# Two kv products one slot later, and a split of a small load, in a linear-attention and MLP kernel

## The chip, the cores and the metric

One core of a Trainium2 chip. The time is device microseconds (us) of one launch; each kernel was launched three times or more, and medians are quoted. Ratios are computed as the mean time of one kernel's runs over the mean time of the other's runs of the same rounds, so they are not quite the ratio of the medians quoted beside them; the bracket is a 95% interval. The experiments ran in three jobs on three chips, so times are compared within a job; traces are compared by times counted from a common event.

A trace is one execution. Times read from a trace count from its first instruction.

## The reference

Eight batches of 576 tokens with eight heads of 64. Per batch and head `kv = k^T v` (64x64), then `out = q kv`, a root-mean-square norm per head times `g_norm`, then a layer norm times `g_ln`, an MLP 512 -> 2048 -> 512 with a ReLU, and a residual:

```python
kv  = einsum('bhsd,bhse->bhde', k, v)
out = einsum('bhsd,bhde->bhse', q, kv)
x   = out / sqrt(mean(out*out, -1) + 1e-6) * g_norm          # then heads side by side: 512 columns
xn  = (x - mean(x)) / sqrt(var(x) + 1e-6) * g_ln
y   = x + relu(xn @ w_ch1) @ w_ch2
```

## The kernel before

TensorE works almost without a pause through the MLPs, `mm1` (into 2048) and `mm2` (back to 512), batch after batch. The attention of later batches is woven in between. The weaving is by hand: an agenda maps slots to pieces of work, and `tick()`, called once per group of MLP matmuls, emits what stands at the current slot. In `mm2` a slot is four 128x512 matmuls. The order so written is the order of the instructions on each engine.

```python
def load_batch(b, *after):                 # GpSimd: the loads of a batch, behind small copies ("gates")
    for element in after:
        nc.gpsimd.tensor_copy(gate, element)
    load(k_in[b % NB], k, b)
    load(v_in[b % NB], v, b)
    load(q_in[b % NB], q, b)

def turn_q_dma(b):                         # transposed q of a batch
    q_p = kv_in.tile(...)
    nc.vector.tensor_copy(q_p..., q_in[b % NB])                        # VectorE, L203
    q_t = qt_pool.tile([128, JJ, HP, 128], bf16, tag="qt", name="qt")
    nc.sync.dma_start_transpose(q_t..., q_p...)                        # SyncE, L205
    qts[b] = q_t

def kv_of(b):                              # 40 small matmuls, L246, then two copies on ScalarE
    ...

class Tile:                                # 128 tokens of one batch
    def o(self): ...                       # TensorE, L271: q (transposed) times kv
    def sq(self): ...                      # ScalarE
    def red(self): ...                     # VectorE; root (rms): ScalarE; y, x, xc: VectorE, xc reads g_ln_sb
    def turn(self, on_pe): ...             # xT: the DMA transpose that mm1 reads, SyncE, L352

# ... cut: the plan of batches 0 to 2 ...
for b in range(3, B):
    s = 32 * b
    at(47 if b == 3 else s - 60,
       lambda b=b: load_batch(b, qts[b - 1][:1, J, HP - 1, 127:],
                              *([blks[2][2][:1, nK - 1, 511:]] if b == 4 else [])))
    d = -41 if b == 3 else -45
    at(s + d, lambda b=b: kv_of(b))
    at(s + d + 1.7, lambda b=b: turn_q_dma(b))
    for j in range(J):
        o = s + d + (11 if b == 3 else 13) + 5 * j
        plan_tile(o, lambda b=b, j=j: main_tile(b, j), o + 6, False)
    if b % 2:
        plan_tile(s - 14, lambda b=b: rem_tile(b), s - 8, False)
    at(s + 14, lambda b=b: rstd_of(b))
```

`plan_tile(s, ...)` puts o, sq and red at slot s, y, x and xc two slots later. "kv 3" below is `kv_of(3)`, "qT 4" the transposed q of batch 4, "the q copy" the VectorE copy ahead of it.

The other place is the load of `g_ln` (512 floats) to four partitions, from which a shuffle spreads it to all:

```python
nc.vector.memset(gl_row, 0.0)
nc.sync.dma_start(
    gl_row[0:128:32, :],
    bass.AP(tensor=moe_g_ln.tensor, offset=moe_g_ln.offset,
            ap=[[0, 4], list(moe_g_ln.ap[0])]))
# ... cut ...
nc.vector.stream_shuffle(g_ln_sb, gl_row, [0] * 32)
```

Of the kernel before, what the change touches and what calls it, by code (L numbers as in the profile page):

```python
# [14 lines left out]
def kernel(  # L15
# [19 lines left out]
    Dm = H * D  # L35
# [48 lines left out]
    gl_row = work.tile([128, Dm], f32, tag="sq", name="gl_row")  # L84
# [11 lines left out]
    def load_batch(b, *after):  # L96
# [5 lines that stand above are left out]
# [15 lines left out]
    def pairs(t, hp0, hp1):  # L117
# [21 lines left out]
    nc.vector.memset(gl_row, 0.0)  # L139
    nc.vector.memset(gn_row, 0.0)  # L140
    nc.sync.dma_start(
        gl_row[0:128:32, :],
        bass.AP(tensor=moe_g_ln.tensor, offset=moe_g_ln.offset,
                ap=[[0, 4], list(moe_g_ln.ap[0])]))
    nc.sync.dma_start(
        gn_row[0:128:32, :],
        bass.AP(tensor=g_norm.tensor, offset=g_norm.offset,
                ap=[[0, 4], list(g_norm.ap[0])]))
# [52 lines left out]
    def turn_q_dma(b):  # L201
        q_p = kv_in.tile([128, JJ, H, D], bf16, tag="qp", bufs=2)
        nc.vector.tensor_copy(q_p.rearrange("p j h d -> p h j d"), q_in[b % NB])  # L203
        q_t = qt_pool.tile([128, JJ, HP, 128], bf16, tag="qt", name="qt")
        nc.sync.dma_start_transpose(  # L205
            q_t.rearrange("p j hp t -> p (j hp) t"), q_p.rearrange("p j h d -> p (j h d)"))
        qts[b] = q_t
# [31 lines left out]
    def kv_of(b):  # L239
        kv_ps = ps_m.tile([128, HP, D], f32, tag="misc", name="kv_ps")  # L240
        kvp = held[b] = kv_pack[b % 4]
        for hp in range(HP):
            for j in range(JJ):
                for hh in range(2):
                    h = 2 * hp + hh
                    nc.tensor.matmul(kv_ps[hh * D:hh * D + D, hp, :],  # L246
                                     lhsT=k_in[b % NB][:, h, j, :], rhs=v_in[b % NB][:, h, j, :],
                                     start=(j == 0), stop=(j == JJ - 1))
        nc.scalar.copy(kvp[:D, :, :D], kv_ps[:D])  # L249
        nc.scalar.copy(kvp[D:, :, D:], kv_ps[D:])  # L250
# [104 lines left out]
    def main_tile(b, j, pool=None, tag="ops"):  # L355
        q_t, kvp = qts[b], held[b]
        if b not in blks:
            blks[b] = new_block("main", 3)
        return Tile([(slice(0, 128), lambda hp: q_t[:, j, hp, :], kvp)], blks[b], j, pool, tag)

    def rem_tile(b):
        mms = []
        for half, bb in enumerate((b - 1, b)):
            qt, kp = qts.pop(bb), held.pop(bb)
            mms.append((slice(half * 64, (half + 1) * 64),
                        lambda hp, qt=qt: qt[:, J, hp, :64], kp))
        if "rem" not in blks:
            blks["rem"] = new_block("rem", 1)
        return Tile(mms, blks["rem"], b // 2)

    def plan_tile(s, make, turn_at, on_pe):
        box = []

        def first():
            t = make()
            box.append(t)
            t.o()
            t.sq()
            t.red()

        def second():
            t = box[0]
            t.y()
            t.x()
            t.xc()

        def third():
            box[0].var()

        def fourth():  # L390
            box[0].turn(on_pe)

        at(s, first)
        at(s + 2, second)
        at(s + 6, third)
        at(turn_at, fourth)
# [22 lines left out]
    def rstd_of(b):  # L419
        rstd = work.tile([128, 4], f32, tag="rstd", bufs=3, name="rstd")  # L420
        nc.scalar.activation(rstd, blks[b][1][:, 2, :], func=AF.Sqrt, scale=1.0 / Dm, bias=eps_sb)  # L421
        nc.vector.reciprocal(rstd, rstd)  # L422
        rstds[b] = rstd
# [45 lines left out]
    def at(slot, fn):  # L469
        agenda.setdefault(int(slot), []).append((slot, fn))  # L470
# [162 lines left out]
# [3 lines that stand above are left out]
           lambda b=b: load_batch(b, qts[b - 1][:1, J, HP - 1, 127:],  # L636
                                  *([blks[2][2][:1, nK - 1, 511:]] if b == 4 else [])))
        d = -41 if b == 3 else -45
        at(s + d, lambda b=b: kv_of(b))
        at(s + d + 1.7, lambda b=b: turn_q_dma(b))  # L640
        for j in range(J):
            o = s + d + (11 if b == 3 else 13) + 5 * j
# [4 lines that stand above are left out]
# [59 lines left out]
```

## Time and profile before

| | before |
|---|---|
| time, median of 3 | 290.73 us (290.61 to 290.76) |
| the execution that was traced | 291.66 us |
| span of that trace | 289.9 us |

From the first part of the page of the kernel before, the span and the busy time of each engine, with its share and its number of instructions:

```profile
span 289.9 us, 5728 instructions
PE 278.9 (96%) x2270; PEld 158.1 (55%) x2295; DVE 149.8 (52%) x331; ACT 153.0 (53%) x333; POOL 41.2 (14%) x69
```

TensorE (PE) is busy for 96% of the span; nothing else comes near. Where it waits is in the table of waits of TensorE (who waited for what, us in all, number of waits, the longest):

```profile
PE even L225 <- DMA v_in<-in_v_dram: 2.0, 1, 2.0
...
PE kv_ps L246 <- DMA v_in<-in_v_dram: 1.0, 2, 0.6
PE p L429 <- issue: 1.0, 6, 0.2
```

After the start there are two waits of kv products for v. The timeline of TensorE (start, duration, engine, line, operation, shapes, count, and the idle time ahead with what ended it; a count at the edge of the window shown is cut off there, so x17 of the 40 matmuls of kv 4) around four places: kv 3, the first o_ps of batch 3, kv 4, and the start of mm1 of batch 3:

```profile
70.86 1.89 PE L429 MATMUL p<-w_sb,m 128*128 128x512 bf16 x8
73.14 0.82 PE L246 MATMUL kv_ps<-v_in,k_in 128*64 128x64 bf16 x40 [0.39 <-DMA v_in<-in_v_dram]
74.12 0.38 PE L429 MATMUL p<-w_sb,m 128*128 128x512 bf16 x1 [0.16 <-issue]
...
82.34 1.91 PE L413 MATMUL p<-xT_blk,w_sb 128*128 128x256 bf16 x16
84.09 0.39 PE L271 MATMUL o_ps<-kv_pack,qt 128*128 128x128 bf16 x4
...
99.38 1.04 PE L429 MATMUL p<-w_sb,m 128*128 128x512 bf16 x4
101.03 0.45 PE L246 MATMUL kv_ps<-v_in,k_in 128*64 128x64 bf16 x17 [0.61 <-DMA v_in<-in_v_dram]
...
113.01 0.39 PE L271 MATMUL o_ps<-kv_pack,qt 128*128 128x128 bf16 x4
113.28 0.38 PE L413 MATMUL p<-xT_blk,w_sb 128*128 128x512 bf16 x1
```

Durations of matmuls overlap here: a 128x512 matmul is given 0.38 us, and in the stream the next one starts 0.216 us later. So starts are to be compared, not ends. (The Trainium skill, "Perfetto Trace Analysis", section "Per-engine timelines", says that the end of a TensorE record is estimated, not observed; the overlap of 0.38 and 0.216 us agrees.) The single records give for kv 3: the matmul before it starts at 72.37, kv 3 at 73.14; where nothing holds up a kv product it starts 0.31 us after the matmul before it, so 0.46 us are lost. kv 4: 100.04 and 101.03, so 0.68 us.

The q copy of batch 4 on VectorE:

```profile
106.63 0.82 DVE L203 COPY q_p<-q_in 128x2560 bf16<-128x2560 bf16 x1
```

and the transposes behind it in SyncE's queue (L205: qT 4; L352: xT of the last tile of batch 3):

```profile
107.51 3.14 SPq L205 DMA_TRANSPOSE qt<-q_p  x1
110.70 1.26 SPq L352 DMA_TRANSPOSE xT_blk<-xc  x1
```

qT 4 lands at 112.59 and is used from 112.80; xT lands at 113.24, and the mm1 matmuls of batch 3 start at 113.28. There is next to no slack in these two (0.21 and 0.04 us).

### The profile page before, as it was taken

How to read it: one execution, taken by the hardware profiler on the slowest of the kernel's cores; microseconds unless marked ns; L12 is line 12 of the kernel's file. 1: busy time of each engine (PE TensorE's matmuls, PEld its weight loads, DVE VectorE, ACT ScalarE, POOL GpSimd, SP SyncE). 2: the span in 40 equal slices, each digit the busy share in tenths (PEclk: the TensorE clock that was granted, in tenths of full speed). 3: DMA queues.
4: the chain of work that ended last, by engine and by line, in shares of the span. 5: the costliest groups of instructions: out<-in, count | busy, mean ns of one | idle time of the engine just before them, and what ended most of it. 6: DMA issues, size and time to landing. Idle time of an engine off the chain costs nothing.

```text
span 289.9 us, 5728 instructions
## 1 busy us (share of the span) xinstructions
PE 278.9 (96%) x2270; PEld 158.1 (55%) x2295; DVE 149.8 (52%) x331; ACT 153.0 (53%) x333; POOL 41.2 (14%) x69
## 2 busy tenths in 40 slices
PE   8789999999999999999999999999999999999994
PEld 3579755995479644445444444444444444444444
DVE  5675119937897783765366925762578200220022
ACT  3467844985369732882288418920894076016400
POOL 8432510041006003200500032000000000000000
PEclk9999999999999999999999999999999999999998
DMA  7999999969786959996994189937202410230033
GB/s 213 198 206 203 199 177 193 221 109 192 138 171 98 198 100 169 196 162 110 158 221 77 39 148 215 156 79 158 55 18 58 107 36 0 45 83 20 0 74 74
DMA packets 67546, 36.76 MB, mean 127 GB/s; under 512 B 35516, under 2 KB 62524, under 8 KB 67520
## 3 DMA queue, kind: packets, MB, share of 16 engines
q0 software_dynamic: 28528, 17.76, 43.6%
q1 hardware_dynamic: 38480, 17.91, 30.3%
q10 hardware_dynamic: 512, 0.72, 0.7%
q8 instruction: 18, 0.29, 0.4%
q14 instruction: 8, 0.07, 0.1%
HBM read 36.71 MB, written 9.44 MB: 159 GB/s over the span
## 4 chain that ended last, share of the span: by engine, by line
PE 69%; DMA 19%; issue 9%; POOL 2%; DVE 0%; POOLq 0%
PE p L429 35%; PE p L413 31%; DMA v_in<-in_v_dram 14%; DMA w_sb<-in_moe_w_ch_dram 5%; PE o_ps L271 2%; PE kv_ps L246 1%; POOL k_in L93 0%; POOL v_in L93 0%; POOL k_in L94 0%; POOL q_in L94 0%; DVE o_sb L434 0%; POOL gate L98 0%; POOLq L93 0%; POOLq L94 0%; POOLq L690 0%
## 5 line engine op out<-in xcount | busy, mean ns | idle before, releaser
L413 PE MATMUL p<-xT_blk,w_sb 128*128 128x128 bf16 (+2 forms) x1017 | 131.3, 285 | 0.8
L429 PE MATMUL p<-w_sb,m 128*128 128x512 bf16 (+2 forms) x591 | 126.6, 368 | 1.5 <-issue 1.0
L416 ACT ACTIVATE m<-p 128x512 bf16<-128x512 f32 x144 | 85.4, 595 | 42.8 <-PE p L413 40.4
L413 PEld LDWEIGHTS <-w_sb 128*128 128x128 bf16 x1024 | 78.7, 98 | 44.5 <-issue 1.1
L429 PEld LDWEIGHTS <-m 128*128 128x128 bf16 x608 | 57.0, 98 | 62.1
L434 DVE SCALAR_TENSOR_TENSOR o_sb<-p,rstd,x_blk 128x512 f32<-128x512 f32 (+2 forms) x38 | 27.3, 720 | 52.9 <-PE p L429 47.3
L277 ACT ACTIVATE sq<-o_ps 128x512 f32<-128x512 f32 x35 | 20.9, 596 | 43.5 <-PE o_ps L271 43.5
L298 DVE TENSOR_REDUCE ss<-sq 128x8 f32<-128x512 f32 x35 | 23.7, 679 | 12.8 <-ACT sq L277 12.6
L340 ACT ACTIVATE dev<-x_blk,st_blk 128x512 f32<-128x512 f32 x36 | 25.7, 714 | 5.7 <-DVE st_blk L326 5.7
L332 DVE SCALAR_TENSOR_TENSOR xc<-x_blk,st_blk,g_ln_sb 128x512 bf16<-128x512 f32 x34 | 25.6, 752 | 1.2
L303 DVE TENSOR_TENSOR y<-o_ps,inv 128x512 f32<-128x512 f32 x33 | 22.8, 692 | 3.4 <-PE p L413 0.5
L322 DVE SCALAR_TENSOR_TENSOR x_blk<-y,g_norm_sb 128x512 f32<-128x512 f32 x33 | 22.8, 691 | 1.1
L315 DVE RECIPROCAL inv<-rms 128x8 f32<-128x8 f32 x36 | 7.2, 201 | 22.9 <-ACT rms L308 22.9
L422 DVE RECIPROCAL rstd<-rstd 128x4 f32<-128x4 f32 x9 | 1.6, 175 | 32.1 <-ACT rstd L421 32.0
L308 ACT ACTIVATE rms<-ss,eps_sb 128x8 f32<-128x8 f32 x36 | 10.7, 296 | 10.6 <-DVE ss L298 10.4
L98 POOL COPY gate<-qt 1x1 bf16<-1x1 bf16 x5 | 0.9, 178 | 106.8 <-DMA qt<-q_p 106.8
L271 PEld LDWEIGHTS <-qt 128*128 128x128 bf16 (+1 forms) x156 | 10.3, 100 | 7.5 <-issue 1.7
L271 PE MATMUL o_ps<-kv_pack,qt 128*128 128x128 bf16 (+1 forms) x156 | 13.6, 220 | 0.0
L198 PE MATMUL p<-fill_sb 128*128 128x512 bf16 x26 | 8.1, 461 | 1.3 <-DVE eps_sb L137 1.2
L246 PEld LDWEIGHTS <-k_in 128*64 128x64 bf16 x280 | 5.0, 112 | 3.7 <-issue 3.6
L249 ACT CAST kv_pack<-kv_ps 64x256 bf16<-64x256 f32 x7 | 2.5, 364 | 8.1 <-PE kv_ps L246 8.1
L340 ACT ACTIVATION_READ_ACCUMULATOR dev<-x_blk,st_blk 128x1 f32 x36 | 6.8, 189 | 0.0
(80 smaller groups left out, 110.9 us busy)
## 6 DMA issues: line engine op xcount, KB each, us to landing
out_dram<-o_sb SPq DMA_DIRECT2D x70, 128.0 KB, 2.5
w_sb<-in_moe_w_ch_dram POOLq DMA_DIRECT2D x8, 512.0 KB, 14.7
q_in<-in_q_dram POOLq DMA_DIRECT2D x7, 320.0 KB, 12.1
k_in<-in_k_dram POOLq DMA_DIRECT2D x7, 320.0 KB, 5.8
v_in<-in_v_dram POOLq DMA_DIRECT2D x7, 320.0 KB, 8.6
q_in<-in_q_dram POOLq DMA_DIRECT2D x8, 256.0 KB, 12.0
k_in<-in_k_dram POOLq DMA_DIRECT2D x7, 256.0 KB, 6.7
v_in<-in_v_dram POOLq DMA_DIRECT2D x7, 256.0 KB, 10.0
```

The lines of the kernel that those rows point to most:

```text
L271: nc.tensor.matmul(flat[rows, hp * 128:(hp + 1) * 128], lhsT=lhsT_of(hp), rhs=kvp[:, hp, :], start=True, stop=True)
L277: nc.scalar.activation(self.sq_t, self.o_ps, func=AF.Square)
L298: nc.vector.tensor_reduce(self.ss, self.sq_t, axis=AX.X, op=ALU.add)
L303: nc.vector.tensor_mul(self.y_t, self.o_ps, self.inv().to_broadcast([128, H, D]))
L308: nc.scalar.activation(self.r, self.ss, func=AF.Sqrt, scale=1.0 / D, bias=eps_sb)
L322: nc.vector.scalar_tensor_tensor(x_blk[:, ts].rearrange("p (h d) -> p h d", h=H), in0=self.y_t, scalar=1.0, in1=g_norm_sb.to_broadcast([12 ...
L332: nc.vector.scalar_tensor_tensor(self.xc_t, in0=x_blk[:, self.ts], scalar=st[:, 1, self.ts:self.ts + 1], in1=g_ln_sb, op0=ALU.add, op1=ALU ...
L340: nc.scalar.activation(dev, x_blk[:, ts], func=AF.Square, bias=st[:, 1, ts:ts + 1], accum_out=st[:, 2, ts:ts + 1])
L413: nc.tensor.matmul(p1[:, i, :], lhsT=w1_sb[:, kk, de * 128:(de + 1) * 128], rhs=blk[2][:, kk, sl], start=(kk == 0), stop=(kk == nK - 1))
L416: nc.scalar.activation(m1[:, de0:de0 + per, sl], p1, func=AF.Relu)
L429: nc.tensor.matmul(p2[:, c0:c1], lhsT=m1s[b][:, de, ts * 128:(ts + 1) * 128], rhs=w2_sb[:, de, c0:c1], start=(de == 0), stop=(de == nDe - 1))
L434: nc.vector.scalar_tensor_tensor(o_sb[:, c0:c1], in0=p2[:, c0:c1], scalar=rstds[b][:, ts:ts + 1], in1=blks[b][0][:, ts, c0:c1], op0=ALU.mu ...
```

## The change

The intent: spare TensorE the two waits for v, by putting four more MLP matmuls ahead of kv 3 and kv 4; and let the small load run on more descriptors.

```diff
     nc.sync.dma_start(
-        gl_row[0:128:32, :],
+        gl_row[0:128:32, :].rearrange("p (c n) -> p c n", c=4),
         bass.AP(tensor=moe_g_ln.tensor, offset=moe_g_ln.offset,
-                ap=[[0, 4], list(moe_g_ln.ap[0])]))
+                ap=[[0, 4], [Dm // 4, 4], [1, Dm // 4]]))
@@
         d = -41 if b == 3 else -45
-        at(s + d, lambda b=b: kv_of(b))
+        at(s + d + (1 if b < 5 else 0), lambda b=b: kv_of(b))
```

## The prediction

> **What bounds the kernel.** TensorE. The profile's first part has it busy 278.9 of 289.9 us; the table of waits gives it little idle time: 2.0 us at the start for batch 0's v, 1.2 for a memset, and 1.0 in two waits of the kv products of batches 3 and 4 (L246) for v_in.
>
> **What the change does.**
> 1. g_ln. I compared the two built programs: the DMA is the same instruction in both, 4 rows of 512 contiguous floats; the build folds the four pieces of 128 back together. So I expect no split: four packets of 2048 bytes again. (Before, the completion counter steps once at 2.80 us and four times from 6.10 to 7.03, so four engines carry it. The Trainium skill, "DMA: Bandwidth & Descriptors", section "Why a DMA increments its semaphore by 16 and not by 1", takes the engine count from the slowest dimension, here 4; a real split would stay on four engines.) Nor is g_ln urgent: its shuffle ends at 8.65 us, its first reader starts at 14.34. Cost: 0.
> 2. kv of batches 3 and 4 each move behind four 128x512 matmuls (0.216 us each in the chain: 0.87 us), to a boundary of an output tile. On ScalarE one rms moves ahead of the kv copies; VectorE, SyncE and GpSimd keep their order.
>
> **kv 3.** In the timeline the matmul before it starts at 72.37. Unstalled kv 5 and 6 start 0.31 after theirs, so it could start at 72.68; it starts at 73.14, after v_in landed at 73.00: 0.46 us lost. One slot later it would be reached at 73.54: no wait. TensorE is then 0.46 us earlier.
>
> **kv 4.** Reached at 100.35, started at 101.03 (0.68 lost), v_in landed 100.89. Its load is released by the transpose of batch 2's last tile (landing 88.98), behind a VectorE/SyncE sequence that runs back to back from about 68 us and hardly waits for TensorE. So I expect that landing near 100.9 still. TensorE would reach the new place at 100.35 - 0.46 + 0.87 = 100.76, still wait about 0.3 us, and be 0.87 us ahead in work done.
>
> **What takes some back.** mm1 of batch 3 starts at 113.28, released by a transpose (xT of its tile 3) landing at 113.24; transposed q of batch 4 lands 112.59, used at 112.80. Both have almost no slack. They hang on VectorE's copy of q (ends 107.46), then SyncE's 3.1 us transpose issue. From about 87 us VectorE waits for rms on ScalarE, which waits for TensorE, so I estimate that copy 0.3 to 0.5 us earlier, not 0.87. So a new wait of about 0.4 us at 112.5, and the net gain is the copy's shift: about 0.45 us. Later stages have slack (v_in of batch 5 lands 126.68, used 130.45).
>
> **Predicted:** 290.25 us, 8 in 10 within 289.6 to 290.7. Faster by over 2%: 0.01; within 2%: 0.98; slower: 0.01.
>
> **Checks in the profile.** Four 2048-byte packets for g_ln. kv 3 no wait; kv 4 a wait of 0.1 to 0.5 us on v_in; a new wait of some tenths before mm1 of batch 3; from there on everything about 0.45 us earlier.
>
> **What would make it wrong.** The load of batch 4 follows TensorE (gain still capped by the transpose near 113 us). VectorE's q copy does not move: gain under 0.1 us. It moves fully: 0.9 to 1.1 us. The split is real on the chip: some 0.1 us lost.

## The result, and the profile after

| | before | after |
|---|---|---|
| time, median of 4 each | 290.67 us (290.46 to 290.76) | 290.60 us (290.33 to 290.80) |
| ratio to before | | 0.9998 [0.9981, 1.0015] |
| the traced execution | 291.66 us | 290.60 us |
| span of the trace | 289.9 us | 288.8 us |
| first kv matmul of batch 0 | 9.02 | 8.34 |
| first mm1 matmul of batch 3 | 113.28 | 112.25 |
| from there to the end of the last eviction | 173.2 | 173.2 |

The timed runs show no difference. The two traces show 1.1 us. A reader who compares only the traces would report a gain that the clock does not see. From the page after, span and busy time, as shown for before:

```profile
span 288.8 us, 5753 instructions
PE 280.9 (97%) x2295; PEld 157.9 (55%) x2295; DVE 149.8 (52%) x331; ACT 153.2 (53%) x333; POOL 41.0 (14%) x69
```

TensorE's waits after:

```profile
PE even L225 <- DMA v_in<-in_v_dram: 1.5, 1, 1.5
...
PE p L413 <- DMA xT_blk<-xc: 0.2, 1, 0.2
```

The line for kv products is gone, as intended. A new line has come, mm1 (L413) waiting for xT. The timeline of TensorE at the same four places:

```profile
70.98 1.89 PE L429 MATMUL p<-w_sb,m 128*128 128x512 bf16 x8
72.81 0.82 PE L246 MATMUL kv_ps<-v_in,k_in 128*64 128x64 bf16 x40
73.56 1.04 PE L429 MATMUL p<-w_sb,m 128*128 128x512 bf16 x4
...
82.13 0.93 PE L413 MATMUL p<-xT_blk,w_sb 128*128 128x256 bf16 x7
83.11 0.40 PE L271 MATMUL o_ps<-kv_pack,qt 128*128 128x128 bf16 x4
...
98.40 1.90 PE L429 MATMUL p<-w_sb,m 128*128 128x512 bf16 x8
100.23 0.82 PE L246 MATMUL kv_ps<-v_in,k_in 128*64 128x64 bf16 x40
...
111.63 0.40 PE L271 MATMUL o_ps<-kv_pack,qt 128*128 128x128 bf16 x4
112.25 1.46 PE L413 MATMUL p<-xT_blk,w_sb 128*128 128x512 bf16 x6 [0.23 <-DMA xT_blk<-xc]
```

kv 3 and kv 4 follow the matmuls before them with no idle time. The q copy of batch 4, and the transposes behind it:

```profile
105.65 0.82 DVE L203 COPY q_p<-q_in 128x2560 bf16<-128x2560 bf16 x1
```

```profile
106.53 3.10 SPq L205 DMA_TRANSPOSE qt<-q_p  x1
109.69 1.26 SPq L352 DMA_TRANSPOSE xT_blk<-xc  x1
```

And the chain of waits after, the stretch that holds the answer (start, duration, what):

```profile
76.11 0.75 DVE o_sb L434
76.86 0.73 DVE q_p L203
77.59 0.50 DVE ss L298
78.09 4.97 DMA qt<-q_p
...
83.11 0.40 PE o_ps L271 x4
...
101.06 7.03 PE p L429 x32
108.08 1.55 SPq L205
...
109.69 2.52 DMA xT_blk<-xc
...
112.25 1.89 PE p L413 x8
```

The chain enters from VectorE, not from TensorE: an eviction, the q copy of batch 3, a reduction, then the DMA transpose of q (qT 3, landing 83.06), which releases the o_ps matmuls of batch 3 at 83.11. At its end it comes to SyncE and xT, which release mm1 at 112.25. One step of it is not to be taken at its word: the tool leads from SyncE (L205) back to a TensorE matmul that ended at 108.08, but SyncE had begun to issue that transpose at 106.53. SyncE's table of waits from 97 to 114 us names what the transpose had waited for, the q copy, which ended at 106.47:

```profile
SPq L205 <- DVE q_p L203: 2.2, 1, 2.2
```

So mm1 hangs on the q copy through SyncE. The input of xT had been ready since 102.52, when VectorE finished its xc; it was issued at 109.69 because it stands behind qT 4 in SyncE's queue (issuing it ahead of qT 4 was not tried). kv 3 is not on the chain; kv 4 stands in the part left out, as work (at 100.30), with no wait ahead of it.

The 1.1 us of the traces come in two parts. 0.68 us were there at the first kv matmul: batch 0's v landed at 8.98 before and at 8.30 after. All of the rest, 0.35 us, lies between that matmul and the first mm1 matmul of batch 3 (104.26 us before, 103.91 after). After it, both kernels take 173.2 us to the end of the last eviction, and so does every kernel below, to 0.01 us. So the whole is about that one stretch, and I call it **the stretch**.

### The profile page after: what moved, and what is told of

Its sections match the earlier page's. It is cut to its first block, busy times and chain, and to the rows that moved or that the text cites. A ratio compares the mean times of both kernels' runs of the same rounds, so it can differ in the third digit from the quotient of the medians.

```text
span 288.8 us, 5753 instructions
## 1 busy us (share of the span) xinstructions
PE 280.9 (97%) x2295; PEld 157.9 (55%) x2295; DVE 149.8 (52%) x331; ACT 153.2 (53%) x333; POOL 41.0 (14%) x69
## 3 DMA queue, kind: packets, MB, share of 16 engines
q1 hardware_dynamic: 38480, 17.91, 31.2%
## 4 chain that ended last, share of the span: by engine, by line
PE 85%; DMA 5%; DVE 5%; ACT 2%; issue 1%; SPq 1%; DVEq 0%; POOLq 0%
PE p L413 41%; PE p L429 37%; PE o_ps L271 2%; DMA v_in<-in_v_dram 2%; DMA qt<-q_p 2%; PE kv_ps L246 2%; DMA xT_blk<-xc 1%; DVE ss L298 1%; ACT m L416 1%; DVE x_blk L322 1%; DVE y L303 1%; DVE o_sb L434 1%; PE p L198 1%; SPq L205 1%; ACT rms L308 0%
## 5 line engine op out<-in xcount | busy, mean ns | idle before, releaser
L413 PE MATMUL p<-xT_blk,w_sb 128*128 128x128 bf16 (+2 forms) x1024 | 131.6, 286 | 0.6 <-DMA xT_blk<-xc 0.2
L429 PE MATMUL p<-w_sb,m 128*128 128x512 bf16 (+2 forms) x608 | 129.1, 368 | 0.0
L413 PEld LDWEIGHTS <-w_sb 128*128 128x128 bf16 x1024 | 78.7, 98 | 44.9 <-issue 1.5
L249 ACT CAST kv_pack<-kv_ps 64x256 bf16<-64x256 f32 x7 | 2.6, 366 | 7.7 <-PE kv_ps L246 7.7
```

Source lines behind the costliest of these rows:

```text
L413: nc.tensor.matmul(p1[:, i, :], lhsT=w1_sb[:, kk, de * 128:(de + 1) * 128], rhs=blk[2][:, kk, sl], start=(kk == 0), stop=(kk == nK - 1))
L429: nc.tensor.matmul(p2[:, c0:c1], lhsT=m1s[b][:, de, ts * 128:(ts + 1) * 128], rhs=w2_sb[:, de, c0:c1], start=(de == 0), stop=(de == nDe - 1))
```

## The experiments

Twelve runs followed, ten of new kernels and one more each of before and after, each with 5 rounds of timing beside the kernel before. To read the traces I took from each one the time that TensorE lost at six places in the stretch. Each is the distance in time of a few weight loads around the place, less the smallest such distance of all kernels. This table is worked out from the traces, in us. Its entries are good to about 0.03 us, and the sums were taken before rounding. What remains of the stretch without the sum is 102.9 to 103.3 us in every kernel; the differences in it lie between 38 and 42 us, in part at kv of batch 1, which waits for its own v in some of the traces and which no edit touches.

```
                wait of TensorE for               evic-   transposes              the    time
kernel          v at kv 3   qT 3   v at kv 4      tion    qT 4     xT     sum   stretch  median  ratio [95%]
before            0.43      0.00     0.66         0.00    0.00    0.04   1.14   104.26   (traced execution 291.66)
before_again      0.00      0.21     0.54         0.00    0.00    0.14   0.89   103.84   290.66  0.9989 [0.9977, 1.0002]
after             0.00      0.22     0.00         0.00    0.28    0.39   0.89   103.91   290.60  0.9998 [0.9981, 1.0015]
after_again       0.00      0.22     0.00         0.00    0.28    0.41   0.91   104.00   290.52  0.9996 [0.9983, 1.0009]
gl_split          0.00      0.24     0.00         0.00    0.25    0.44   0.92   103.88   290.55  0.9996 [0.9984, 1.0009]
kv3_only          0.00      0.23     0.39         0.00    0.00    0.28   0.90   104.19   290.70  1.0001 [0.9989, 1.0014]
kv4_only          0.17      0.04     0.00         0.00    0.26    0.42   0.89   104.02   290.67  0.9999 [0.9985, 1.0012]
q4_only           0.00      0.25     0.41         0.00    0.00    0.00   0.65   103.69   290.34  0.9992 [0.9979, 1.0004]
q4_first          0.00      0.22     0.00         0.17    0.00    0.00   0.39   103.32   290.09  0.9969 [0.9957, 0.9981]
kv4_q4            0.00      0.21     0.00         0.03    0.00    0.00   0.25   103.25   290.03  0.9981 [0.9967, 0.9995]
q4_after_osb      0.00      0.23     0.00         0.00    0.00    0.00   0.23   103.16   289.79  0.9972 [0.9960, 0.9985]
q4_osb_o3         0.00      0.00     0.19         0.00    0.00    0.00   0.20   103.15   289.81  0.9975 [0.9960, 0.9989]
both_fixed        0.00      0.00     0.02         0.48    0.00    0.00   0.50   103.45   290.60  0.9986 [0.9971, 1.0002]
kv_earlier        1.59      0.49     1.49         0.00    0.93    0.41   4.91   108.04   294.09  1.0099 [1.0083, 1.0116]
```

The kernel before in the three jobs had medians of 290.97 (before_again, both_fixed, q4_first, kv_earlier), 290.53 (q4_only, after_again, kv4_q4, q4_after_osb) and 290.52 us (the other four).

### before_again: the kernel before, once more

No edit.

> The kernel before, unchanged, for the spread. Theory A (given back): the two kv waits are there in every execution, and the change removes them, but most of it comes back as waits for transposed q and xT, leaving about 0.35 us; the other 0.68 us of the profile's 1.05 us was an earlier start by luck (batch 0's v landed 8.30 instead of 8.98). Theory B (luck): the kv waits of the profile before belong to that one slow execution (291.66 us, about 1 us above its timed runs), and a typical execution hardly has them. A: kv 3 and kv 4 each lose 0.3 to 0.8 us here too, whenever batch 0's v lands. B: together under 0.3 us. Both: time ratio 1.000 within 0.001.

In this trace kv 3 did not wait: v of batch 3 landed at 71.71, and kv 3 started at 71.96, 0.31 us after the matmul before it. kv 4 still waited. TensorE's timeline at kv 3, the first o_ps of batch 3, kv 4 and mm1 of batch 3, and the q copy:

```profile
71.96 0.82 PE L246 MATMUL kv_ps<-v_in,k_in 128*64 128x64 bf16 x40
...
83.12 0.40 PE L271 MATMUL o_ps<-kv_pack,qt 128*128 128x128 bf16 x4
...
99.95 0.82 PE L246 MATMUL kv_ps<-v_in,k_in 128*64 128x64 bf16 x40 [0.49 <-DMA v_in<-in_v_dram]
...
112.30 1.46 PE L413 MATMUL p<-xT_blk,w_sb 128*128 128x512 bf16 x6
```

```profile
105.66 0.82 DVE L203 COPY q_p<-q_in 128x2560 bf16<-128x2560 bf16 x1
```

Set beside the lines of after: qT 3 releases its o_ps at 83.12 here and 83.11 there; the q copy of batch 4 starts at 105.66 here and 105.65 there; mm1 starts at 112.30 here and 112.25 there. A before of ordinary speed and after have the same stretch, 103.84 and 103.91 us. This gives theory A the part about giving back (0.54 us at kv 4, gone in after, come again as qT 4 and xT), and theory B the part about luck for kv 3 alone: its 0.46 us belonged to that execution. Neither theory as written holds in full. My number under A, "kv 3 and kv 4 each lose 0.3 to 0.8 us here too", was wrong for kv 3. The ratio of the kernel to itself, 0.9989, missed the 1.000 within 0.001 by a hair: it is a measure of the noise, and a ratio as near to 1 as that shows nothing.

### q4_first and both_fixed: take away what gives the gain back

q4_first is the changed kernel with the q copy of batch 4 moved ahead of the remainder tile on VectorE:

```diff
-        at(s + d + 1.7, lambda b=b: turn_q_dma(b))
+        at(s + d + (0.9 if b == 4 else 1.7), lambda b=b: turn_q_dma(b))
```

> The changed kernel with the copy of batch 4's q ahead alone. A: the wait at the start of mm1 of batch 3 (0.6 us in the profile after) is gone, that of 0.3 us at batch 3's first o_ps stays: 0.8 us faster than before, 289.8 us, ratio 0.997. B: ratio 0.999 to 1.000.

The copy began at 102.99 instead of 105.65, the waits for qT 4 and xT are gone from the table, and the time fell clear of the noise. Against before_again, the same kernel as before in the same job, it fell by 0.57 us, and the stretch by 0.52. The wait for qT 3 stayed at 0.22 us, as expected.

both_fixed is q4_first with one more slot before the first tile of batch 3:

```diff
-            plan_tile(o, lambda b=b, j=j: main_tile(b, j), o + 6, False)
+            plan_tile(o + (1 if (b, j) == (3, 0) else 0), lambda b=b, j=j: main_tile(b, j), o + 6, False)
```

> The changed kernel, with the copy of batch 4's q put ahead of the remainder tile on VectorE (so its transpose is issued about 2.7 us earlier), and the first attention tile of batch 3 one slot later. A: the waits that gave the gain back (0.3 us at the first o_ps of batch 3, 0.6 us at the start of mm1 of batch 3) are gone, and nothing new takes them; the whole 1.1 us is kept: 289.5 us, ratio 0.996. B: no wait to remove in typical runs: ratio 0.999 to 1.000.

Missed. The wait for qT 3 is gone, but a new one has come, for the eviction of an output tile on VectorE. TensorE's timeline of both_fixed:

```profile
104.92 0.59 PE L429 MATMUL p<-w_sb,m 128*128 128x512 bf16 x2 [0.32 <-DVE o_sb L434]
```

The eviction (o_sb) stands behind the q copy on VectorE, and the q copy waited there 0.90 us for q to land. q4_first has the same in small, 0.17 us. "Nothing new takes them" was the wrong part of my expectation.

### kv_earlier: the opposite of the change

```diff
-        at(s + d, lambda b=b: kv_of(b))
+        at(s + d - (1 if b < 5 else 0), lambda b=b: kv_of(b))
```

> The kernel before with kv of batches 3 and 4 one slot (0.87 us) earlier, the opposite of the change: the suspected waits made longer. A: kv 3 waits 0.87 us more, all else follows; kv 4 stays pinned to its load: 0.8 to 1.0 us slower in all, 291.6 us, ratio 1.003. B: the waits are mostly slack in typical runs: 0 to 0.4 us slower, ratio up to 1.0015.

Missed by far, and on the slow side: 3.1 us slower in the medians, 1% in the ratio. So the places of the kv products do count, in the other direction. kv 3 waited 1.59 us, more than A's 0.87 and the wait before together (0.87 to 1.30), and kv 4 waited 1.49. What A lacked is what a waiting kv product does to ScalarE: its two copies (L249, L250) stand in ScalarE's queue ahead of the rms of the next attention tiles. ScalarE at kv 4 in kv_earlier:

```profile
102.65 0.36 ACT L249 CAST kv_pack<-kv_ps 64x256 bf16<-64x256 f32 x1 [1.68 <-PE kv_ps L246]
...
103.42 0.49 ACT L308 ACTIVATE rms<-ss,eps_sb 128x8 f32<-128x8 f32 x2
```

and VectorE, which needs that rms:

```profile
103.75 0.20 DVE L315 RECIPROCAL inv<-rms 128x8 f32<-128x8 f32 x1 [2.07 <-ACT rms L308]
```

ScalarE sat idle 1.68 us for kv 4 while the input of the rms had been ready since 101.69, when VectorE's reduction ended; VectorE lost 2.07 us. (The Trainium skill, "Perfetto Trace Analysis", section "Per-engine timelines", calls ScalarE and VectorE strict FIFO; this is such a case, with its price.) The q copy of batch 4 began at 109.59 instead of 105.66, and 1.34 us of waits for qT 4 and xT follow from it (0.93 + 0.41). In before, the first of these rms ran at 100.10, ahead of the kv copies (101.88), and VectorE did not wait.

### q4_only, after_again, kv4_q4: which of the two limits, and does kv 3 count

q4_only is the edit of q4_first made to the kernel before. after_again is the changed kernel once more, with no edit. kv4_q4 is the kernel before with kv 4 alone moved and the q copy ahead:

```diff
-        at(s + d, lambda b=b: kv_of(b))
-        at(s + d + 1.7, lambda b=b: turn_q_dma(b))
+        at(s + d + (1 if b == 4 else 0), lambda b=b: kv_of(b))
+        at(s + d + (0.9 if b == 4 else 1.7), lambda b=b: turn_q_dma(b))
```

> The kernel before (kv at its old places) with the copy of batch 4's q ahead, the edit of q4_first without the change. Theory C (the later of two): mm1 of batch 3 starts at the later of TensorE's own arrival, which the wait of kv 4 delays, and the transposes behind batch 4's q copy; before, both come within 0.1 us of each other, so that either cure alone is worth nothing and both together 0.6 to 0.9 us. C: 0 to 0.3 us faster than before, ratio 0.999 to 1.000, and the kv 4 wait of about 0.5 us still there. Rival D (the q copy alone was the limit, kv never mattered): as fast as q4_first, ratio 0.997.

> The changed kernel, unchanged, in one job with the others. C: no wait at kv 3 and kv 4, a wait of about 0.6 us in all before mm1 of batch 3, total 0 to 0.3 us faster than before, ratio 0.999 to 1.000. D: the same.

> kv of batch 4 alone later, and the copy of batch 4's q ahead; kv 3 at its old place. C: what kv 3 waits (0 or 0.46 us in the two traces of before) is given back at the first o_ps of batch 3, which needs the transposed q of batch 3, so the part of kv 3 is worth nothing: as fast as q4_first, ratio 0.997 (0.9965 to 0.998). Rival E (kv 3 counts too): only half of the gain, ratio 0.9985.

q4_only came out as theory C says: kv 4 waits 0.41 us, mm1 does not wait, ratio 0.9992. after_again did too: ratio 0.9996. Rival D fell: its 0.997 lies outside the interval of q4_only, [0.9979, 1.0004]. Neither edit alone shows a gain that the intervals can tell from zero, and both together, in q4_first and kv4_q4, do. kv4_q4's trace has the stretch of q4_first (103.25 and 103.32 us) with kv 3 at its old place, so kv 3's part is worth nothing in this state. Its ratio, 0.9981, lies between what C and E gave; the interval holds both, so for kv 3 it is the traces that decide, not the clock.

### kv3_only and kv4_only: each half of the move

Both start from the kernel before, so `g_ln` is loaded as there: kv3_only has `(1 if b == 3 else 0)` and kv4_only `(1 if b == 4 else 0)` in place of `(1 if b < 5 else 0)`.

> The kernel before with kv of batch 3 alone one slot later. C: worth nothing; the wait for kv 4 of about 0.5 us stays, mm1 of batch 3 starts 103.8 to 104.0 us after the first kv matmul as in before_again (103.84), ratio 0.999 to 1.000.

> The kernel before with kv of batch 4 alone one slot later. C: no wait at kv 4, and what it waited (0.5 us) appears before mm1 of batch 3 for the transposed q of batch 4 and xT; mm1 of batch 3 starts 103.8 to 104.0 us after the first kv matmul, ratio 0.999 to 1.000.

Both ratios are 1.000 within their intervals. The table's sum is the point: 0.89, 0.89, 0.91, 0.92, 0.90 and 0.89 us in the six kernels from before_again to kv4_only, whichever kv product moved. The same loss is only paid at different places. kv3_only's stretch, 104.19 us, is longer than I expected (103.8 to 104.0) by 0.2 us; its excess lies ahead of kv 3 and at none of the six places. The trace shows where: v of batch 1 landed 30.35 us after the first kv matmul, against 29.36 in before_again, and kv of batch 1 began its weight loads at 30.57, against 30.37. In kv4_only kv 3 waited 0.17 us, and qT 3 then took 0.04 instead of 0.2: what kv 3 loses, qT 3 does not.

### gl_split: the split made real

In the changed kernel the page counts the packets of SyncE's queue as before, 38480. The line of the changed kernel (queue, packets, MB, share of 16 engines):

```profile
q1 hardware_dynamic: 38480, 17.91, 31.2%
```

So the split was folded back in the build, and the first half of the change is no change: the single packets of the load are four of 2048 bytes in both traces. gl_split pads the tile, so that the pieces can't be joined.

```diff
-    gl_row = work.tile([128, Dm], f32, tag="sq", name="gl_row")
+    gl_row = m1pool.tile([128, 4, 136], f32, tag="m1", name="gl_row")
@@
-        gl_row[0:128:32, :].rearrange("p (c n) -> p c n", c=4),
+        gl_row[0:128:32, :, :128],
@@
-    nc.vector.stream_shuffle(g_ln_sb, gl_row, [0] * 32)
+    nc.vector.stream_shuffle(g_ln_sb.rearrange("p (c n) -> p c n", c=4), gl_row[:, :, :128], [0] * 32)
```

> The changed kernel with the split of g_ln made real: gl_row is padded to 136 columns per quarter, so that the build can't fold the pieces; the result stays right. Expected: sixteen packets of 512 bytes in place of four of 2048, still on four engines (the completion counter steps once early and then four times); g_ln's shuffle still long before its first reader at about 14 us; batch 0's v lands within its spread (8.1 to 9.0 us); ratio to before as for the changed kernel, 0.999 to 1.000. Rival F (the split was meant to free the start and does once real): v of batch 0 lands before 8.1 us and ratio under 0.998.

The same line of gl_split:

```profile
q1 hardware_dynamic: 38492, 17.91, 30.6%
```

Twelve more packets: sixteen instead of four. They take 40 ns each instead of 96. The completion counter stepped at 2.87 and then four times, from 6.68 to 6.90 us, so four engines still carried them, as the Trainium skill says ("DMA: Bandwidth & Descriptors", "Why a DMA increments its semaphore by 16 and not by 1": the slowest dimension sets the number of engines). v of batch 0 landed at 8.28, the shuffle began at 7.6 and the first reader of `g_ln` at 13.6 us. Ratio 0.9996: as the changed kernel. Rival F fell.

### q4_after_osb and q4_osb_o3: a version that beats both

q4_after_osb is the changed kernel with the q copy of batch 4 behind the eviction and still ahead of the remainder tile:

```diff
-        at(s + d + 1.7, lambda b=b: turn_q_dma(b))
+        at(s + d + (1.2 if b == 4 else 1.7), lambda b=b: turn_q_dma(b))
@@
-            plan_tile(s - 14, lambda b=b: rem_tile(b), s - 8, False)
+            plan_tile(s - (13.5 if b == 3 else 14), lambda b=b: rem_tile(b), s - 8, False)
```

> As q4_first, but with the copy of batch 4's q behind the eviction of the first output tile of batch 2 and still ahead of the remainder tile. In q4_first's trace the output tile was evicted later and TensorE lost 0.17 us there. C: that loss goes, the rest stays: 0.1 to 0.2 us faster than q4_first, ratio to before 0.9965.

VectorE runs the eviction, then the copy, with no idle time ahead of it (q4_first lost 0.56 us there waiting for q to land), and mm1 starts at 111.31, not 112.25 (103.16 instead of 103.91 us after the first kv matmul):

```profile
102.17 0.75 DVE L434 SCALAR_TENSOR_TENSOR o_sb<-p,rstd,x_blk 128x512 f32<-128x512 f32 x1
102.83 0.82 DVE L203 COPY q_p<-q_in 128x2560 bf16<-128x2560 bf16 x1
```

```profile
111.31 2.32 PE L413 MATMUL p<-xT_blk,w_sb 128*128 128x512 bf16 x10
```

Median 289.79 against 290.53 of the kernel before in the same rounds, ratio 0.9972 [0.9960, 0.9985]. The expected step of 0.1 to 0.2 us from q4_first is there in the traces (103.32 to 103.16), too small for the clock across two jobs. q4_osb_o3 is q4_after_osb with the slot of both_fixed as well:

> q4_after_osb with the first attention tile of batch 3 one slot later, to take away the wait of 0.3 us for the transposed q of batch 3 that is left. If nothing else takes it: mm1 of batch 3 starts 102.9 us after the first kv matmul (103.16 in q4_after_osb), ratio 0.9965. As in both_fixed it may come back as a late eviction on VectorE: then 103.2 to 103.5 and ratio 0.9975 to 0.9985.

The wait for qT 3 is gone (0.23 to 0.00) and kv 4, now reached earlier, waits 0.19 us for v. The stretch stays at 103.15. Neither of my two reasons held: the wait came back, but at v of batch 4, not as an eviction. The best version found is q4_after_osb, with or without that slot.

## Why the prediction was right or wrong

The measured 290.60 us lies inside the range of 289.6 to 290.7, and "within 2%" was right. The forecast gain of about 0.45 us did not come; 0.07 us between medians is inside the noise. That the range held is in part luck: no change at all, 290.67, lies in it too, by 0.03 us.

- **g_ln is no change.** Right. The split was folded in the build, four packets of 2048 bytes, and gl_split shows that a real one costs and gains nothing either.
- **kv 3: "0.46 us lost".** The reading of the trace was right and its use was wrong. The traced execution was 291.66 us long, above all timed runs, and I took its late v for the usual one. In before_again kv 3 waits nothing, and in kv4_only 0.17 us. I had both numbers, 291.66 and 290.73, before I predicted.
- **kv 4: "still wait about 0.3 us".** Wrong: no wait in after. v of batch 4 landed at 99.69 there, not near 100.9. In the other traces it landed at 99.5 to 100.1, except in before (100.89) and kv_earlier (101.66). That the load would not follow TensorE was right: counted from the first kv matmul, v landed at 91.36 in before_again and at 91.35 in after, and at 91.87 in the slow trace that I read.
- **"What takes some back": the new wait before mm1 of batch 3.** The mechanism was right, in place and in kind; the size was not: about 0.4 us forecast, 0.28 for qT 4 and 0.39 for xT in after. Of these 0.67 us an ordinary before already has 0.14, so the change added 0.53, and that is all of the 0.54 us that it takes away at kv 4. The experiments show it: with the q copy ahead, both go and the time falls.
- **"that copy 0.3 to 0.5 us earlier".** This is the term of the sum that was mis-sized. Against a before of ordinary speed the copy begins 0.01 us earlier (105.65 and 105.66; counted from the first kv matmul, 0.10 us later), so the net gain, which I had set equal to the copy's shift, is nothing. The step that I missed is the wait for qT 3 at 83.1 us. It holds TensorE to VectorE's pace, 30 us ahead of the place where I looked: TensorE waits there 0.21 to 0.25 us wherever kv 3 did not wait and the tile stood at its old place, so of a loss at kv 3 only what exceeds about 0.22 us counts. In kv4_only it is 0.17, in before_again nothing, so removing it gains nothing, and VectorE's later work, which was to move with it, does not move. In before itself that wait was 0.00, hidden behind the late kv 3, so the trace could not show it as a wait; the landing of qT 3 at 83.84 and its use at 83.98 would have shown it as missing slack, and I checked such slack only for batch 4.
- **The 0.35 us between the two traced stretches** is near the forecast, but it compares a late execution of before with a common one of after. The predicted mechanism did act on that pair: kv 3 had lost 0.43 us there, about 0.2 more than qT 3 gives back, and the q copy of batch 4 began 97.61 us after the first kv matmul in before and 97.31 in after, 0.30 us earlier, as forecast. The pair is not the kernels.

What stays open: why batch 0's v landed between 8.10 and 8.98 us, and batch 3's v between 70.7 and 73.0, in executions of kernels whose loads up to there are the same. No experiment addressed it. The traces show where the lateness sits. Each of these loads counts sixteen completions. In before the fourteenth came at 8.14 for batch 0 and at 71.53 for batch 3, the last at 8.98 and 73.00; in before_again the fourteenth came at 8.11 and 71.08, the last at 8.41 and 71.71. So mostly the last one or two of the sixteen were late; for batch 3 the load was also issued 0.54 us later in before.

## What to carry to other kernels

A wait on the busiest engine is worth only what lies between it and the next thing that the engine waits for, or nearly waits for: before removing one, list the later inputs that arrive with little slack, and follow each to the engine that makes it. Here a loss of 0.9 us was moved between five places and not reduced, until the copy that holds up the last two of them was moved ahead of work that was not needed yet, the remainder tile's. And set the traced execution's own time against the timed runs first: a trace that is 1 us slow will show waits that the kernel does not usually have.

## What the Trainium skill lacked or had wrong

- No page says that the build joins access patterns that are contiguous: four pieces of 128 floats came out as four packets of 2048 bytes, 38480 packets in the queue before and after, and 38492 once the pieces were padded apart.
- No page warns of missing matmul records; the pages on the notification queue say only in general that records can be lost when a queue is full. The traces of before, gl_split, kv3_only, kv4_only and q4_osb_o3 show waits of 0.2 us "<-issue" in TensorE's table that the others don't have; before has 2270 matmul records and 2295 weight loads, after has 2295 of both. Between the weight loads at these places there is no such pause, so these waits (1.0 us in before) are holes in the record.
- "Perfetto Trace Analysis" gives no spread between executions: thirteen of the fourteen traces began kv of batch 0 between 8.1 and 8.6 us, before at 9.02, and that is 0.68 us of the 1.1 us between the two first traces.
- "DMA: Bandwidth & Descriptors", section "Latency and other measured facts", has two of the sixteen DMA engines usually slower than the rest. In before fourteen increments for batch 0's v came by 8.14 and two at 8.68 and 8.98; in after all sixteen came by 8.30. So the difference is there in one execution and hardly in another, in keeping with the page's "usually"; the trace does not name the engines.
- The same section gives the DMA transpose a bandwidth of 261 GB/s, measured on one kernel whose middle dimension was not contiguous, and more for a contiguous one. A q transpose here (128 x 2560 in 2 bytes, 655 KB) took 5.05 us from issue to landing, 106.53 to 111.58 in after, or 130 GB/s with its fixed costs, and held SyncE's queue for 3.1 us. The second number, which delays xT behind it, is on no page as a time; the same page only counts the sequencer's cycles of transposes of other sizes, for earlier generations of the chip, in a part on trn3.
